# Block-sparse attention with a gated output layer: rebuilt on head pairs over 128 partitions, with the gate's convolution as matrix products

## The chip, the cores and the metric

One NeuronCore of one Trainium2 chip runs the program. It has four engines that compute: TensorE (PE; its weight loads are shown apart as PEld), VectorE (DVE), ScalarE (ACT) and GpSimd (POOL). SyncE (SP) issues the transfers between DRAM and the on-chip memory SBUF. Matrix products land in PSUM, eight banks of 128 partitions x 2 KB, from which DVE and ACT read. The metric is the device time of one execution in microseconds. TensorE's clock has two levels, 1.2 and 2.4 GHz; the profile prints the granted share, 0.50 or 1.00, or a mean over a stretch.

## The reference, cut to what matters

```python
# q, k, v: (4, 8, 768, 64); chunks of 32 keys, so 24 chunks; 6 are kept for each query
k_min, k_max = min and max of k over each chunk
ub = sum over d of maximum(q * k_min, q * k_max)          # a bound per query and chunk
ub = where(chunk is not in the future, ub, -1e9)
top_chunks = argsort(ub)[..., -6:]
scores = q @ k.T / 8
mask = (key's chunk in top_chunks) & (key is not in the future)
attn = softmax(where(mask, scores, -1e9)); x = attn @ v    # heads side by side: (4, 768, 512)
# then, on x
gate_pre = sum over k in 0..4 of conv_w[k] * x shifted by 4-k rows   # causal convolution per channel
out = (sigmoid(gate_pre) * (x @ w_val)) @ w_out            # 512 x 512 each
```

## The kernel before

The kernel walks over 16 pairs of heads (4 batches, 4 pairs each). For a pair, `p13_k` transposes the keys of each head on TensorE, 64 columns at a time (12 float32 transposes, L165), copies them to float16 on ACT (L167) and takes the minimum and maximum of each chunk on DVE (L169, L173). `p13_q` transposes the queries (12 more, L195) and writes each result three times from ACT: as it is, with negative values cut off, and as float16 (L197, L199, L201). The bound is then one float32 product per head and query tile (L205, 12 products of 24 columns, each of which runs as two rows of the profile).

`p48_a` adds the causal fill (L213), finds the eight largest values (L216) and compares with the sixth (L221, on POOL for one head and on DVE for the other). `p48_b` transposes the choice (`selT`, L241, L244) into 24 further rows of the contraction, so that a chunk that is not kept gets -30. `qk` computes the scores as 24 products of 256 columns into banks `psbg` (L255), takes the exponential on ACT 512 columns at a time (L259, 12 per pair), and multiplies the diagonal blocks with a mask on DVE (L262, L264). `av` multiplies with the values (L273, 42 products per pair), and for each of the 12 query tiles divides by the sum (L277, L278, DVE). Six float32 transposes (L302) and two ACT copies (L304) write `xT`.

The gated layer follows per batch: `moe_gate` is the convolution, one product and four multiply-adds of 768 elements on DVE (L314, L318), then the sigmoid on ACT (L322); `moe_val` (L331, L336) and `moe_out` (L344, L350, L351) are the two 512 x 512 layers. They are handed out over the pairs that follow the batch; what is left of the last batch runs at the end.

Buffers come from tile pools, and a scheduler of the framework sets the order on each engine and puts in the waits. Every engine works through its own queue in order, so a waiting instruction holds all behind it. The four banks `psbg` serve transposes, scores and both layers in turn.

## Time and profile before

| | before |
|---|---|
| three timed runs, us | 481.65, 481.69, 481.94 (median 481.69) |
| profiled execution, first to last instruction | 479.9 us |
| PE busy | 366.2 us, 76% |
| DVE busy | 342.4 us, 71% |
| ACT busy | 291.3 us, 61% |
| POOL busy | 42.5 us, 9% |

The profile is of one execution, and its span runs from the first to the last instruction; the page gives no other time of that execution. The median of the timed runs is 1.8 us above the span. Busy time of PE holds the modelled ends of pipelined products, so that start-to-start distances in the timeline price a product better than the mean length of one. The granted clock is read by stretch, since it moves between its two levels many times.

### The profile page before, as it was taken

The page shows a single profiled execution, that of the slowest core. Times are in us where ns is not written, and L with a number is a line of the kernel's source. Part 1 is how long each engine was busy: PE and PEld are TensorE (multiplying, and loading weights), DVE is VectorE, ACT ScalarE, POOL GpSimd, SP SyncE. Part 2 cuts the span into 40 slices and gives each one's busy share as a digit, 9 for nine tenths or more (in the row PEclk, how much of TensorE's full clock was granted, in tenths as well). Part 3 has the DMA queues.
Part 4 walks back from the last instruction along what each step waited for, and adds up shares of the span by engine and source line. Part 5 has one row for each costly group of instructions (what it writes and reads, how often), then busy time and mean ns, then how long its engine had stood idle before and what let it go on. Part 6 is the DMA issues. An engine that isn't in the chain of part 4 may idle for free.

```text
span 479.9 us, 7043 instructions
## 1 busy us (share of the span) xinstructions
PE 366.2 (76%) x2240; PEld 256.1 (53%) x2240; DVE 342.4 (71%) x1345; ACT 291.3 (61%) x548; POOL 42.5 (9%) x132
## 2 busy tenths in 40 slices
PE   0589797888688778778977878777877858587794
PEld 0467576666465646545645556545545645364441
DVE  0465967677796668889577869789786777857671
ACT  3665664556677346767565756576767765662742
POOL 0012010200100101100100102010101001010000
PEclk9955955555565657868587657859796756657588
DMA  7973221212120041203123040303232000000023
GB/s 195 206 141 57 47 54 34 66 33 67 33 68 0 3 98 34 66 20 108 29 87 87 1 99 17 85 1 102 63 100 66 1 1 1 1 0 23 23 89 132
DMA packets 83173, 28.08 MB, mean 59 GB/s; under 512 B 78688, under 2 KB 79040, under 8 KB 83136
## 3 DMA queue, kind: packets, MB, share of 16 engines
q1 hardware_dynamic: 83136, 27.63, 24.0%
q8 instruction: 18, 0.29, 0.3%
q14 instruction: 19, 0.16, 0.1%
HBM read 21.33 MB, written 6.29 MB: 58 GB/s over the span
## 4 chain that ended last, share of the span: by engine, by line
PE 54%; DVE 21%; ACT 16%; issue 4%; SPq 2%; DMA 1%; ACTq 0%; DVEq 0%
PE ps_ub L205 13%; PE psbg L255 12%; PE psbg L331 5%; PE ps_av L273 5%; PE psbg L344 5%; PE psbg L195 4%; ACT PT L259 4%; DVE gp L318 3%; ACT aq L199 3%; DVE onat L278 3%; PE pst L165 3%; PE psbg L302 3%; ACT aq L197 3%; DVE uth L244 2%; PE psbg L241 2%
## 5 line engine op out<-in xcount | busy, mean ns | idle before, releaser
L259 ACT ACTIVATE PT<-psbg 128x512 f16<-128x512 f32 x192 | 101.8, 609 | 55.1 <-PE psbg L255 52.6
L255 PE MATMUL psbg<-uth,KE 88*128 88x256 f16 x384 | 95.1, 392 | 17.6 <-DVE uth L244 8.1
L273 PEld LDWEIGHTS <-PT 128*128 128x128 f16 x672 | 57.2, 120 | 46.9 <-issue 33.6
L205 PEld LDWEIGHTS ps_ub<-kmmc,aq 128*128 128x128 f32 x384 | 71.2, 282 | 14.6 <-ACT aq L199 7.1
L273 PE MATMUL ps_av<-vaug,PT 128*128 128x65 f16 x672 | 65.5, 222 | 16.8 <-DVE onat L278 15.6
L205 PE MATMUL ps_ub<-kmmc,aq 128*128 128x24 f32 x384 | 73.0, 343 | 6.8 <-DVE kmmc L183 3.4
L255 PEld LDWEIGHTS <-KE 88*128 88x128 f16 x384 | 48.6, 137 | 39.6 <-issue 24.0
L318 DVE SCALAR_TENSOR_TENSOR gp<-xT,cwT,gp 128x768 f32<-128x768 f16 x64 | 64.8, 1012 | 0.7
L277 DVE RECIPROCAL rcp<-ps_av 128x1 f32<-128x1 f32 x192 | 32.0, 167 | 43.6 <-PE ps_av L273 40.6
L195 PE MATMUL psbg<-ident,qnat 128*64 128x128 f32 x192 | 43.0, 349 | 19.2 <-DVE kmn L173 6.6
L197 ACT ACTIVATE aq<-psbg 64x384 f32<-64x384 f32 x64 | 30.9, 482 | 38.6 <-PE psbg L195 27.3
L278 DVE TENSOR_SCALAR onat<-ps_av,rcp 128x64 f32<-128x64 f32 x192 | 52.9, 276 | 1.3
L221 POOL TENSOR_SCALAR selpair<-mub,top 128x24 f32<-128x24 f32 x96 | 32.7, 353 | 174.2 <-DVE top L216 173.7
L244 DVE TENSOR_SCALAR uth<-psbg 24x384 f16<-24x384 f32 x64 | 35.3, 551 | 17.6 <-PE psbg L241 16.1
L195 PEld LDWEIGHTS psbg<-ident,qnat 128*64 128x64 f32 x192 | 22.4, 138 | 33.6 <-issue 8.4
L165 PE MATMUL pst<-ident,knat 128*64 128x128 f32 x96 | 21.1, 330 | 24.9 <-DMA qnat<-in_q_dram 15.3
L302 PE MATMUL psbg<-ident,onat 128*128 128x128 f32 x96 | 35.2, 384 | 3.7 <-DVE onat L278 3.3
L331 PE MATMUL psbg<-xT,wval_sb 128*128 128x384 f16 x128 | 34.6, 416 | 2.6 <-ACT xT L304 1.8
L344 PE MATMUL psbg<-wout_sb,gv 128*128 128x512 f16 x96 | 31.2, 446 | 5.4 <-ACT xT L304 4.7
L304 ACT ACTIVATE xT<-psbg 128x384 f16<-128x384 f32 x32 | 15.7, 489 | 28.7 <-PE psbg L302 26.8
L199 ACT ACTIVATE aq<-psbg 64x384 f32<-64x384 f32 x64 | 30.9, 484 | 0.7
L350 ACT ACTIVATE osb<-psbg 128x512 f32<-128x512 f32 x24 | 14.2, 595 | 27.1 <-PE psbg L344 21.7
(40 smaller groups left out, 468.1 us busy)
## 6 DMA issues: line engine op xcount, KB each, us to landing
knat<-in_k_dram SPq DMA_DIRECT2D x32, 192.0 KB, 3.0
qnat<-in_q_dram SPq DMA_DIRECT2D x32, 192.0 KB, 3.1
vnat<-in_v_dram SPq DMA_DIRECT2D x32, 192.0 KB, 3.0
out_dram<-osb SPq DMA_DIRECT2D x24, 256.0 KB, 2.0
w<-in_moe_w_val_dram SPq DMA_DIRECT2D x1, 1024.0 KB
w<-in_moe_w_out_dram SPq DMA_DIRECT2D x1, 1024.0 KB
KE<-echunk SPq DMA_DIRECT2D x4, 36.0 KB
cwT<-in_moe_conv_w_dram SPq DMA_DIRECT2D x5, 2.0 KB, 6.4
```

Source lines behind the costliest of these rows:

```text
L195: nc.tensor.transpose(out=pt[0:64, tl * 128:(tl + 1) * 128], in_=qnat[:, hh, t, :], identity=ident)
L197: nc.scalar.activation(out=aq[64:128, hh, w * 384:(w + 1) * 384], in_=pt[0:64, 0:384], func=AF.Copy)
L199: nc.scalar.activation(out=aq[0:64, hh, w * 384:(w + 1) * 384], in_=pt[0:64, 0:384], func=AF.Relu)
L205: nc.tensor.matmul(out=ps_ub[:, hh, it * NCH:(it + 1) * NCH], lhsT=aq[:, hh, it * 128:(it + 1) * 128], rhs=kmm[:, hh], start=True, stop=True)
L255: nc.tensor.matmul(out=pq[:, half * 256:(half + 1) * 256], lhsT=ke[:, hh, jt * 128:(jt + 1) * 128], rhs=uth[:, hh, w * 256:(w + 1) * 256], ...
L259: nc.scalar.activation(out=pw[:, 2 * a:2 * a + 2, :].rearrange("p a b -> p (a b)"), in_=pq[:, :], func=AF.Exp)
L273: nc.tensor.matmul(out=pav, lhsT=pw[:, jt, qh * 128:(qh + 1) * 128], rhs=vaug[:, hh, jt, :], start=(jt == 0), stop=(jt == qt))
L278: nc.vector.tensor_scalar(out=onat[:, qt, hh * 64:(hh + 1) * 64], in0=pav[:, 0:D], scalar1=r, scalar2=None, op0=ALU.mult)
L302: nc.tensor.transpose(out=pt[:, qtl * 128:(qtl + 1) * 128], in_=onat[:, qt, :], identity=ident)
L318: nc.vector.scalar_tensor_tensor(out=gp, in0=xT[:, slot, ki:ki + S], scalar=cwT[:, ct, ki:ki + 1], in1=gp, op0=ALU.mult, op1=ALU.add)
L331: nc.tensor.matmul(out=pv[:, 0:384], lhsT=wval_sb[:, ct, et * 128:(et + 1) * 128], rhs=xT[:, slot0 + ct, 4 + sw * 384:4 + (sw + 1) * 384], ...
L344: nc.tensor.matmul(out=po[:, :], lhsT=gv_tiles[et][:, sti * 128:(sti + 1) * 128], rhs=wout_sb[:, et, :], start=(et == 0), stop=(et == NCT ...
```

## The change

A pair of heads now lies side by side in 128 partitions. Six transposes bring the keys of both heads, six the queries. ACT writes one float32 copy of the queries; POOL makes the two float16 copies and DVE the one without negative values. The bound is a product with a block matrix `KB` that holds both heads (48 columns), in two parts that add up in PSUM, for 5 of 6 query tiles, since the first tile has no more than four chunks to choose from. The choice is one comparison of 240 columns, and its transposes are float16.

Scores are packed so that nearly all columns are causal ones: 10 banks of 512 columns and one of 256 per pair, in three banks of their own (`ps_s`). The diagonal blocks are cleared by POOL (`affine_select`) and no longer by DVE. The result of `av` fills one bank per head and is divided by two instructions. The transposes to `xT` are float16, and DVE copies them.

The convolution is 20 products of 384 columns per channel block, with diagonal matrices that hold each weight as a float16 high part and a float16 rest; POOL builds them once. The sigmoid is written with tanh. The output layer's factor 0.5 sits in the last copy.

Three stages run side by side: attention of pair i, choice of pair i+1, keys and queries of pair i+2; `merge` spreads their steps. Keys and queries of the first pair are loaded ahead of the other inputs, and the weights are cast on POOL.

```diff
     nc.sync.dma_start(out=ident, in_=ident_dr.ap())
+    load_kq(0)
+    for i in range(3):
+        for hh in range(2):
+            nc.sync.dma_start(out=KE[i][HP[1 - hh], hh, :], in_=e_dr.ap())
+    nc.sync.dma_start(out=cfill, in_=cfill_dr.ap())
...
+        def khalf(w):
+            pt = bank([128, HB])
+            for tl in range(3):
+                nc.tensor.transpose(out=pt[:, tl * 128:(tl + 1) * 128],
+                                    in_=kn[:, 3 * w + tl, :], identity=ident)
+            sl = slice(w * HB, (w + 1) * HB)
+            for hh in range(2):
+                nc.scalar.activation(out=ke[HP[hh], hh, sl], in_=pt[HP[hh]],
+                                     func=AF.Copy, scale=0.125)
+            cs = slice(w * 12, (w + 1) * 12)
+            ptc = pt.rearrange("p (c t) -> p c t", t=CH)
+            nc.vector.tensor_reduce(out=kmx[:, cs], in_=ptc, axis=AX.X, op=ALU.max)
...
+            sl = slice(w * HB, (w + 1) * HB)
+            nc.scalar.activation(out=q32[:, sl], in_=pt, func=AF.Copy)
+            for hh in range(2):
+                nc.gpsimd.tensor_copy(out=qu[HP[hh], hh, sl], in_=q32[HP[hh], sl])
+            a = max(w * HB, 128)
+            nc.vector.tensor_scalar(out=rq[:, a:(w + 1) * HB], in0=q32[:, a:(w + 1) * HB],
+                                    scalar1=0.0, scalar2=None, op0=ALU.max)
+
+        def vcast():
+            for hh in range(2):
+                nc.gpsimd.tensor_copy(out=va[:, hh, :, 0:D],
+                                      in_=vn[:, :, hh * 64:(hh + 1) * 64])
...
+            for it in range(1, NT):
+                ts = slice(it * 128, (it + 1) * 128)
+                nc.tensor.matmul(out=pu[:, it - 1, :], lhsT=rq[:, ts], rhs=kb[:, 0, :],
+                                 start=True, stop=False)
+                nc.tensor.matmul(out=pu[:, it - 1, :], lhsT=q32[:, ts], rhs=kb[:, 1, :],
+                                 start=False, stop=True)
+            nc.vector.tensor_tensor(out=mub.rearrange("p i c -> p (i c)"),
+                                    in0=pu.rearrange("p i c -> p (i c)"),
+                                    in1=cfill, op=ALU.add)
...
+        def cmp():
+            nsv = ns.rearrange("p i (s c) -> p i s c", s=2)
+            nc.vector.tensor_tensor(
+                out=nsv[:, :, :, 0:NCH],
+                in0=mub.rearrange("p i (s c) -> p i s c", s=2),
+                in1=top8[:, :, :, 5:6].to_broadcast([128, SELT, 2, NCH]),
+                op=ALU.is_lt)
...
+            pt = bank([128, SELT * 128], F16)
+            for i in range(SELT):
+                nc.tensor.transpose(out=pt[:, i * 128:(i + 1) * 128], in_=ns[:, i, :],
+                                    identity=identh)
+            for hh in range(2):
+                nc.vector.tensor_copy(out=qu[CP[hh], hh, 128:S], in_=pt[CP[hh], :])
...
+    BANKS = [
+        [(0, 0, 256, 512)],
+        [(0, 0, 0, 256), (256, 4, 512, 256)],
+        [(0, 1, 256, 512)],
+        [(0, 1, 128, 128), (128, 3, 384, 384)],
+        [(0, 2, 256, 512)],
+    ]
...
+        def tri(pt, col, n):
+            ap = pt[:, col:col + n * 128].rearrange("p (a b) -> p a b", a=n)
+            nc.gpsimd.affine_select(out=ap, in_=ap, pattern=[[0, n], [1, 128]],
+                                    compare_op=ALU.is_ge, fill=0.0, base=0,
+                                    channel_multiplier=-1)
+
+        def score(hh, bi):
+            pq = bank([128, 512], FP, "s", 3)
+            for col, jt, q0, n in BANKS[bi]:
+                nc.tensor.matmul(out=pq[:, col:col + n],
+                                 lhsT=ke[KP[hh], hh, jt * 128:(jt + 1) * 128],
+                                 rhs=qu[KP[hh], hh, q0:q0 + n], start=True, stop=True)
+            pt = ppool.tile([128, 512], F16, tag=f"P{hh}{bi}", name=f"P{hh}{bi}")
+            nc.scalar.activation(out=pt, in_=pq, func=AF.Exp)
+            for part in BANKS[bi]:
+                keep(hh, pt, *part)
+            if bi == 1:
+                ap = pt.rearrange("p (a b) -> p a b", a=2)[:, :, 0:128]
+                nc.gpsimd.affine_select(out=ap, in_=ap, pattern=[[0, 2], [1, 128]],
+                                        compare_op=ALU.is_ge, fill=0.0, base=0,
...
+        def av(hh):
+            pav = bank([128, NT, D + 1], FP, "av", 2)
...
+                    nc.tensor.matmul(out=pav[:, qt, :], lhsT=where[hh, jt, qt],
+                                     rhs=va[:, hh, jt, :], start=(jt == 0), stop=(jt == qt))
+            nc.vector.reciprocal(out=rcp[:, hh, :], in_=pav[:, :, D])
+            nc.vector.tensor_tensor(
+                out=onat[:, :, hh * 64:(hh + 1) * 64], in0=pav[:, :, 0:D],
+                in1=rcp[:, hh, :].unsqueeze(2).to_broadcast([128, NT, D]), op=ALU.mult)
...
+            pt = bank([128, S], F16)
+            for qt in range(NT):
+                nc.tensor.transpose(out=pt[:, qt * 128:(qt + 1) * 128], in_=onat[:, qt, :],
+                                    identity=identh)
+            nc.vector.tensor_copy(out=xT[:, slot, 4:4 + S], in_=pt)
...
-        gp = mpool.tile([128, S], FP, tag=f"gp{ct}", name=f"gp{ct}")
-        nc.vector.tensor_scalar(
-            out=gp, in0=xT[:, slot, 0:S], scalar1=cwT[:, ct, 0:1],
-            scalar2=None, op0=ALU.mult)
-        for ki in range(1, KSZ):
-            nc.vector.scalar_tensor_tensor(
-                out=gp, in0=xT[:, slot, ki:ki + S], scalar=cwT[:, ct, ki:ki + 1],
-                in1=gp, op0=ALU.mult, op1=ALU.add)
-        g = mpool.tile([128, S], FP, tag=f"gate{ct}", name=f"gate{ct}")
-        nc.scalar.activation(out=g, in_=gp, func=AF.Sigmoid)
-        gate_tiles[ct] = g
+        g = mpool.tile([128, S], FP, tag=f"g{ct}", name=f"g{ct}")
+        for w in range(2):
+            pg = bank([128, HB])
+            n = 0
+            for ki in range(KSZ):
+                for part in range(2):
+                    nc.tensor.matmul(out=pg, lhsT=diag[:, ki * NCT + ct, part, :],
+                                     rhs=xT[:, slot, w * HB + ki:w * HB + ki + HB],
+                                     start=(n == 0), stop=(n == 2 * KSZ - 1))
+                    n += 1
+
+            nc.scalar.activation(out=g[:, w * HB:(w + 1) * HB], in_=pg, func=AF.Tanh, scale=0.5)
...
+    def moe_weights():
+        nc.gpsimd.tensor_copy(out=wval_sb, in_=w32[:, 0])
+        nc.gpsimd.tensor_copy(out=wout_sb, in_=w32[:, 1])
...
+        for ki in range(KSZ):
+            i = ki * NCT + ct
+            for part, w in ((0, cwT), (1, cwl)):
+                nc.gpsimd.tensor_scalar(out=diag[:, i, part, :], in0=identh,
+                                        scalar1=w[:, i:i + 1], scalar2=None, op0=ALU.mult)
...
+    merge(kq_steps(0))
+    merge(sel_steps(0), kq_steps(1))
+    for i in range(NPAIR):
+        if i + 2 < NPAIR:
+            load_kq(i + 2)
+            load_v(i + 2)
+        merge(attn_steps(i),
+              sel_steps(i + 1) if i + 1 < NPAIR else [],
+              kq_steps(i + 2) if i + 2 < NPAIR else [],
+              moe[i])
...
```

On PE, around the bound's products of one pair in mid-kernel, before (`ps_ub` is the bank of the bound, `KE` and `uth` are operands of the scores):

```order
L255 MATMUL psbg1_102<-uth_2101,KE0_79 128x256
L195 MATMUL psbg3_104<-ident_70,qnat_2091 64x128 x3
...
L255 MATMUL psbg0_101<-uth_2101,KE0_79 128x256
L205 MATMUL ps_ub_105<-kmmc_2405,aq_2400 128x24 x9
L255 LDWEIGHTS KE0_79
L255 MATMUL psbg3_104<-uth_2101,KE0_79 128x256
```

The same place in the changed kernel, where L207 and L209 alternate five times (`ps_w` are the three common banks, `KB` the block matrix of both heads):

```order
L314 MATMUL ps_w_2653<-identh_74,onat_2419 128x128
L155 MATMUL ps_w_2683<-ident_73,kn_2661 128x128 x3
L207 MATMUL ps_w_2697<-KB1_95,rq_2427 128x48
L209 MATMUL ps_w_2697<-KB1_95,q32_2426 128x48
...
L348 LDWEIGHTS wval_sb_76
L348 MATMUL ps_w_2710<-xT_84,wval_sb_76 128x384
...
L348 MATMUL ps_w_2716<-xT_84,wval_sb_76 128x384
...
L271 MATMUL ps_s_2740<-QU1_89,KE1_86 128x512
```

Nine products of 24 columns (of the pair's twelve) stood between scores; now ten of 48 columns stand between transposes and the value layer.

On POOL, one pair of the changed kernel (`P` are exponentials, `QU` the float16 queries, `VA` the float16 values); before, this engine had two MEMSETs and six TENSOR_SCALARs of 24 columns per pair:

```order
L280 AFFINE_SELECT P01_1218<-P01_1218 128x2x128
L264 AFFINE_SELECT P03_1240<-P03_1240 128x256
L264 AFFINE_SELECT P04_1253<-P04_1253 128x128
L264 AFFINE_SELECT P5_1265<-P5_1265 128x256
L183 CAST QU0_88<-q32_1201 64x384 x2
L190 CAST VA1_92<-vn_1412 128x6x64
L280 AFFINE_SELECT P11_1337<-P11_1337 128x2x128
L264 AFFINE_SELECT P13_1352<-P13_1352 128x256
L183 CAST QU0_88<-q32_1201 64x384 x2
L264 AFFINE_SELECT P14_1365<-P14_1365 128x128
```

Masks that the products of `av` wait for now share one queue with casts for a later pair.

On ACT, around a gate, before (`gp` is the convolution):

```order
L201 ACTIVATE uth<-psbg_102 64x384
L322 ACT_TABLE_LOAD
L322 ACTIVATE gate_1238<-gp_1232 128x768
L259 ACT_TABLE_LOAD
L259 ACTIVATE PT_0_1097<-psbg_101 128x512
```

and in the changed kernel, which has one table load in all:

```order
L181 ACTIVATE q_1677<-ps_w 128x384
L275 ACTIVATE P_1842<-ps_s 128x512
L339 ACTIVATE g_1845<-ps_w 128x384 x2
L275 ACTIVATE P_1932<-ps_s 128x512
```

The table loads around a gate are gone, and the gate reads PSUM.

## Rows read from the trace of the kernel before

**Rows 1.** The page: busy time, share of the span and instructions of each engine.

```profile
PE 366.2 (76%) x2240; PEld 256.1 (53%) x2240; DVE 342.4 (71%) x1345; ACT 291.3 (61%) x548; POOL 42.5 (9%) x132
```

**Rows 2.** Stretches: from:to, length, busy us of PE, PEld, DVE, ACT, POOL, clock, DMA.

```profile
41.30:460.40 419.10, 331.67 (x2069) 231.74 (x2069) 319.41 (x1275) 264.70 (x502) 38.80 (x116) 0.66 0.18 44
346.30:360.00 13.70, 10.02 (x85) 6.54 (x84) 12.17 (x38) 8.89 (x19) 0.94 (x2) 1.00 0.38 108
360.00:363.40 3.40, 1.38 (x10) 0.91 (x9) 3.33 (x6) 3.33 (x7) 0.00 (x0) 1.00 0.79 201
363.40:377.00 13.60, 12.67 (x67) 9.25 (x68) 8.70 (x49) 9.35 (x18) 2.06 (x6) 0.50 0.03 7
458.90:472.00 13.10, 12.31 (x70) 6.35 (x69) 8.60 (x15) 5.39 (x8) 0.00 (x0) 1.00 0.27 104
```

**Rows 3.** Timeline of PE: start us, length us, engine, line, operation, out<-in, shape, count.

```profile
254.93 0.49 PE L195 MATMUL psbg<-ident,qnat 128*64 128x128 f32 x3
255.26 0.27 PE L255 MATMUL psbg<-uth,KE 88*128 88x256 f16 x1
257.67 4.04 PE L205 MATMUL ps_ub<-kmmc,aq 128*128 128x24 f32 x18 [0.63 <-ACT aq L199]
...
274.38 0.36 PE L273 MATMUL ps_av<-vaug,PT 128*128 128x65 f16 x6
274.57 0.27 PE L165 MATMUL pst<-ident,knat 128*64 128x128 f32 x1
...
336.55 2.19 PE L205 MATMUL ps_ub<-kmmc,aq 128*128 128x24 f32 x18 [0.63 <-ACT aq L199]
...
468.00 5.34 PE L344 MATMUL psbg<-wout_sb,gv 128*128 128x512 f16 x24
```

**Rows 4.** Groups of ACT: line, operation, shapes, count | busy us, mean ns | idle before, releaser.

```profile
L259 ACT ACTIVATE PT<-psbg 128x512 f16<-128x512 f32 x192 | 101.8, 609 | 55.1 <-PE psbg L255 52.6 <-ACT xT L304 0.9 <-PE ps_av L273 0.8
L322 ACT ACT_TABLE_LOAD x13 | 16.7, 1283 | 0.2
L304 ACT ACTIVATE xT<-psbg 128x384 f16<-128x384 f32 x32 | 15.7, 489 | 28.7 <-PE psbg L302 26.8 <-PE ps_av L273 1.6
L167 ACT ACTIVATE KE<-psbg 64x384 f16<-64x384 f32 x32 | 14.6, 481 | 17.2 <-PE psbg L165 13.4 <-DVE gv L336 3.3 <-DVE kmx L169 0.4
```

**Rows 5.** Groups of DVE, in the same columns.

```profile
L318 DVE SCALAR_TENSOR_TENSOR gp<-xT,cwT,gp 128x768 f32<-128x768 f16 x64 | 64.8, 1012 | 0.7
L216 DVE MAX8 top<-mub 128x8 f32<-128x24 f32 x192 | 22.8, 170 | 0.0
L169 DVE TENSOR_REDUCE kmx<-psbg 64x12 f32<-64x384 f32 x32 | 17.3, 541 | 2.1 <-ACT KE L167 2.1
L336 DVE TENSOR_TENSOR gv<-psbg,gate 128x384 f16<-128x384 f32 x32 | 17.2, 549 | 2.1 <-PE psbg L331 1.9
L213 DVE TENSOR_TENSOR mub<-ps_ub,cfill 128x144 f32<-128x144 f32 x32 | 9.0, 301 | 28.2 <-PE ps_ub L205 28.2
```

**Rows 6.** The value cast on DVE, all instructions: ns min/median/max; its longest in the timeline.

```profile
L154 DVE TENSOR_SCALAR vaug<-vnat x32: 339/347/548, 17.7 to 408.8; 128x384 f16<-128x384 f32 x32
...
57.41 0.55 DVE L154 TENSOR_SCALAR vaug<-vnat 128x384 f16<-128x384 f32 x1
...
57.68 0.51 POOL L159 MEMSET selpair<- 128x240 f32 x1
```

**Rows 7.** Groups of POOL, in the columns of rows 4.

```profile
L221 POOL TENSOR_SCALAR selpair<-mub,top 128x24 f32<-128x24 f32 x96 | 32.7, 353 | 174.2 <-DVE top L216 173.7
L158 POOL MEMSET selpair<- 128x240 f32 x16 | 4.8, 298 | 209.3 <-PE psbg L241 159.9 <-DVE PT L264 35.1 <-DVE uth L244 14.0
```

**Rows 8.** The chain that ended last, in order of time; last, a row of the timeline.

```profile
15.35 1.46 PE pst L165 x6
...
41.24 1.59 PE psbg L255 x6
...
460.46 0.49 ACT L304 ACTIVATE xT<-psbg 128x384 f16<-128x384 f32 x1
```

447 lines of the change are left out of this document (174 added, 273 removed).

## The prediction

> **What bounds the kernel now.** I read the page's busy times first, then the stretches with their clock, then the timeline of PE. On the page no engine is full: PE 76%, DVE 71%, ACT 61% [rows 1]. The stretches tell why. Between the first score and the last `xT`, 419 us for 16 pairs or 26.2 us each, the mean clock is 0.66 [rows 2], so (1 - 0.66)/0.5 = 68% of that time is at half clock. In a stretch at half clock PE is busy 12.67 of 13.60 us (93%) and DVE only 8.70. In one at full clock it is the other way: DVE 12.17 of 13.70 (89%), PE 10.02. In the 3.4 us after it DVE and ACT are both busy for 3.33 us, PE for 1.38, and then the clock is down [rows 2]. So two limits take turns: at half clock PE sets the pace; at full clock DVE with ACT does, PE runs thin, and the clock falls again. In the tail, where long products follow one another (PE 12.31 of 13.10 us), it stays at 1.00 [rows 2].
>
> Prices of PE at full clock come from start-to-start distances [rows 3]. A float32 transpose: (255.26 - 254.93)/3 = 0.110 us. A product of `av` with 65 columns: (274.57 - 274.38)/6 = 0.032. The 24 products of 512 columns at the end: 5.34/24 = 0.222, or 0.434 ns a column; shorter float16 products are priced by columns. A row of the bound: 2.19/18 = 0.122, and 4.04/18 = 0.224 at half clock.
>
> A pair before is then 36 transposes 3.96, 24 rows of the bound 2.93, scores 24 x 256 columns 2.67, `av` 42 x 0.032 = 1.34, value layer 8 x 384 columns 1.33, output layer 6 x 0.222 = 1.33: 13.6 us at full clock, 27.1 at half. DVE has 319.4/16 = 20.0 us a pair [rows 2]. With the shares seen, half-clock time costs 27.1/0.93 = 29.2 us a pair and full-clock time 20.0/0.89 = 22.4. Mixing rates, 0.68/29.2 + 0.32/22.4 = 0.0376 pairs per us, or 26.6 us a pair, against 26.2 measured. The same sum serves for the changed kernel.
>
> **The change, PE.** Transposes: 12 float32 ones 1.32, 11 float16 ones of 128 columns at about 0.06 (between `av`'s 0.032 and 0.110) 0.66. Bound: 10 products, 20 rows; at 0.122 they cost 2.44. The columns double, which costs nothing if the weight load of 128 columns covers it, and up to 4.9 if time follows columns; I take 2.44, because 24 columns at 0.434 ns a column would explain only 0.010 of the 0.122. Scores: 5376 columns, 2.33. `av` as before 1.34. Convolution, new: 20 products of 384 columns, 3.33. Value and output layers as before, 1.33 each. Sum 14.1 us a pair, 225 us in all: half a microsecond more than before. The change does not relieve PE; the convolution spends what the transposes save.
>
> **The change, DVE.** Gone: the convolution (four multiply-adds of 1012 ns per block [rows 5]), the masks, the narrow divisions. Left for a pair [rows 5 and 6]: 4 reductions of 541 ns 2.16; 10 MAX8 1.70; the fill and the comparison, 240 columns each, between 0.301 and 0.549, at 0.40 each; two copies of the choice with 640 columns, from 0.30 to 0.81 (0.549 and the slope (549 - 301)/240 = 1.03 ns a column), 1.2 for both; 2 divisions 1.1 and 2 reciprocals 0.34; the copy to `xT`, 0.55 to 0.95, at 0.75; 2 products with the gate 1.1; cut-off queries 0.347 for 384 columns, 0.6 for both; five small ones for `KB` at 0.17 to 0.35, 1.2. Ends 9.6 and 12.5; I take 11.0, against 20.0.
>
> **The change, ACT.** 10 exponentials 6.09, one of 256 columns about 0.4, 4 copies of keys 1.92, 2 of queries 0.98, 2 tanh on 384 columns 0.98 (the copy's row, since no tanh has run), 1.5 output copies 0.91 [rows 4]: 11.3. Gone are two thirds of the copies of queries, the copies to `xT`, and the table loads of 1283 ns around the gates (13 in the row shown, 12 more at L259 going back).
>
> **The change, POOL.** It has 13 wide instructions a pair. The rows know 0.298 us for a 240-column MEMSET and 0.353 for a 24-column compute instruction [rows 7]; masks and casts do not occur. Low end: 13 x 0.298 = 3.9. High end, 0.353 and 298/240 = 1.24 ns for each further column: 0.80 for six casts, 0.64 for five masks of 256, 0.48 for two of 128, or 9.0. I take 8, the compute row being nearer than a MEMSET. The first four pairs carry 40 diagonals (0.48 each, 4.8 a pair) and two weight casts (2.9 each): up to 15 there, level with PE, hidden by the order's slack of three stages, 0.5 to 1 us each if not. DVE and POOL disturb each other: the value cast takes 347 ns as a rule and 548 where a MEMSET of POOL, itself 0.51 instead of 0.298, lies beside it [rows 6 and 7]. Seven DVE instructions a pair (`rq`, comparison, `KB`) could lose 0.2 to 0.8 us when POOL is busy, which is half the time: 0.7 to 2.8, so DVE up to 13.8, still within PE's 14.4 below.
>
> The Trainium skill ("SBUF — State Buffer", Who interferes with whom) calls this an exclusive lock: a DVE instruction in a two-port mode, or with two SBUF inputs, and a GpSimd instruction block one another for a whole instruction. The case of 548 ns agrees; by that rule the upper 2.8 us would hold, and the sum would not move, since PE stays the longest.
>
> **Sum.** At full clock PE is now the busiest (14.1; ACT 11.3, DVE 11, POOL 8), so it is no longer thinned by DVE.
>
> Head: the first transposes start at 15.35 and the first score at 41.24 [rows 8]. Keys and queries are now second in the load queue, so transposes can start near 5.5. From there: 12 transposes at half clock 2.6, the last reductions and `KB` 3.5, cut-off 0.6, bound 20 x 0.224 = 4.5, fill, MAX8, comparison 2.5, transposes and copies 1.8: first score at 21.
> Tail: before, last `xT` at 460.95 to the end at 479.9, 19 us. Now convolution 3.3, value layer 32 x 0.167 = 5.3, output layer 24 x 0.222 = 5.3, and the last copies, stores and hand-overs about 6 (6.6 after the last product before: 473.34 to 479.9): 20.
> Middle: PE's 225 less head (24 transposes, one bound, 5.4) and tail (14.0) is 206, or 12.9 us a pair. At full clock, at the 89% that the pace-setter reached, 14.4 us; at half clock 25.7/0.93 = 27.7. The share of half clock is the unknown, with 0 and 0.68 as ends. I take 0.30: the load that thinned PE halves (20.0 to 11), the bound is 20 rows of 48 columns instead of 24 of 24 before which the clock fell, and each pair has a dense block of 3.3 us like the tail's. Then 0.70/14.4 + 0.30/27.7 = 0.0594, or 16.8 us a pair, 269 for 16.
> 21 + 269 + 20 = 310 us of span. With the 1.8 us by which the median lies above the span: **312 us**. With shares 0 and 0.5 the middle is 230 and 303: 273 to 346 is the forecast's own range.
>
> **Rivals.**
> *The clock stays as it is now.* The bound still stands as one block, and such a block runs thin: 18 rows of 24 columns took 2.19 us at full clock [rows 3], the time of some 5000 columns of the output layer. If each pair's block ends the full clock as before, the share stays 0.68: 21.4 us a pair, 342, total 385. Against it: DVE and ACT no longer fill the full-clock stretches.
> *Hand-overs thin PE.* Three score banks, each held for a product (0.222) and an exponential (0.609 [rows 4]): if PE waits out the difference at 11 banks (4.2 us) and for exponential and mask twice before `av` (2.4 us), a pair at full clock costs 12.9 + 6.6 = 19.5, total 355. For it: ACT waits 52.6 us for scores and DVE long for `av` now; against it: other products stand between the scores in the order.
> *Half clock throughout.* 27.7 x 16 + 43 = 486, slower than before, since PE's columns have not become fewer. It decides only from a share of about 0.99; the tail and every dense stretch speak against it.
> *POOL sets the pace, slower than before.* Its masks stand between exponential and `av`. The middle would have to exceed 482 - 43 = 439 us, 27.4 a pair or 2.1 us for each of 13 instructions, six times the row of 0.353. At 2.3 us: 30 us a pair, 523 in all.
>
> The Trainium skill ("GPSIMD Engine Reference", Elementwise — side-by-side cycle accounting) gives about 12 cycles an element for branching on data, at 1.2 GHz; were the masks such code, 1536 columns a pair would cost an estimated 15.4 us and POOL about 20, a total of 364 (inside the range below). No row here shows a mask on POOL.
>
> **How the numbers follow.** Forecast 0.56; clock as now 0.19; hand-overs 0.17; half clock throughout 0.04; POOL 0.04. A measurement of this kernel tells 0.2%, about 1 us, from no change. Faster: 0.92; slower: 0.07, most of the last two cases; the same: 0.01. The range from 270 to 388 takes in the forecast, the clock's case and the hand-overs, less what the unknown prices add beyond their ends: about 8 in 10.
>
> **What would show it.** Right: a mean clock near 0.85 in the middle, PE above 80% busy, near 17 us from one pair's first score to the next, DVE and ACT each near 11 us a pair, first score near 21 us. Wrong: a mean clock under 0.7; POOL busy above 70% with PE waiting on masks; DVE's mean lengths well above the rows because POOL holds it; rows of the bound at twice 0.122.

## The result and the profile after

The changed kernel takes **293.81 us** (median of 4 runs, 293.45 to 294.23) against 481.81 for the kernel before: a ratio of 0.607 (95% interval 0.604 to 0.610). The forecast was 312 with a range from 270 to 388. The profiled execution has a span of 292.5 us. Runs more than 1.5% above the fastest of their kernel are left out of the medians, ranges and ratios below.

The page of the changed kernel: busy time of each engine with its share of the span, then the granted clock in 40 slices, then the engines' shares of the chain that ended last.

```profile
PE 241.3 (82%) x2161; PEld 171.6 (59%) x2161; DVE 155.2 (53%) x522; ACT 160.2 (55%) x329; POOL 121.8 (42%) x261
...
PEclk9999975956999999999999999999999999999999
...
PE 66%; POOL 12%; ACT 10%; issue 3%; SPq 3%; DVE 2%; DMA 2%; ACTq 0%; POOLq 0%
```

Against [rows 1], DVE fell from 342.4 to 155.2 us, ACT from 291.3 to 160.2, POOL rose from 42.5 to 121.8. PE fell from 366.2 to 241.3, though by the prediction's prices it has half a microsecond more to do in each pair: what fell is the time at half clock.

The stretches of the changed kernel, cut at first scores: the head; pairs 0 and 1 together, then pair 1 alone; pairs 2 to 14; the last pair. Columns as in [rows 2].

```profile
0.00:27.07 27.07, 10.96 (x50) 9.22 (x50) 14.48 (x43) 7.02 (x13) 10.04 (x24) 1.00 1.03 232
...
27.07:73.70 46.63, 27.39 (x218) 18.96 (x219) 15.22 (x61) 17.39 (x36) 37.15 (x68) 0.74 0.58 106
...
48.40:73.70 25.30, 15.18 (x124) 10.27 (x122) 8.31 (x31) 9.30 (x19) 24.69 (x44) 0.69 0.29 63
73.70:260.80 187.10, 175.78 (x1707) 128.40 (x1705) 117.27 (x404) 121.41 (x253) 72.05 (x162) 1.00 0.31 75
...
260.80:273.70 12.90, 12.36 (x113) 7.27 (x110) 3.75 (x9) 8.63 (x17) 2.61 (x7) 1.00 0.22 83
```

The middle is one long stretch at full clock: 13 pairs in 187.1 us, **14.4 us a pair, PE busy 94%** of it (175.78/187.1), DVE 9.0 us a pair, ACT 9.3, POOL 5.5. (A mean: from first score to first score single pairs take 12.4 to 16.9 us, the shortest being the early ones, which have neither value nor output layer yet.) The two limits that took turns in [rows 2] have become one. What is slow now is the beginning: pairs 0 and 1 take 46.6 us, at a mean clock of 0.74, and POOL is busy for 24.69 of the 25.30 us of pair 1.

PE's prices in the middle, at full clock (timeline: start, length, engine, line, operation, out<-in, shape, count; the count's last product ends within the length, so a price is the distance to the next start):

```profile
157.29 2.28 PE L334 MATMUL ps_w<-xT,diag 128*128 128x384 f16 x13
159.41 0.50 PE L314 MATMUL ps_w<-identh,onat 128*128 128x128 f16 x6
...
159.96 0.49 PE L155 MATMUL ps_w<-ident,kn 128*128 128x128 f32 x3
160.29 0.38 PE L271 MATMUL ps_s<-QU,KE 88*128 88x256 f16 x2
...
160.67 0.39 PE L209 MATMUL ps_w<-KB,q 128*128 128x48 f32 x2
```

A product of the convolution costs (159.41 - 157.29)/13 = 0.163 us, a float16 transpose (159.74 - 159.41)/6 = 0.055, a float32 transpose (160.29 - 159.96)/3 = 0.110. From 160.67 to the output layer's product at 162.68 stand 18 rows of the bound: 0.112 each with 48 columns, where rows of 24 columns cost 0.122 before [rows 3].

### The profile page after: what moved, and what is told of

It is laid out like the page before. It is cut to its first block, busy times and chain, and to the rows that moved or that the text cites. A ratio compares the mean times of both kernels' runs of the same rounds, so it can differ in the third digit from the quotient of the medians.

```text
span 292.5 us, 5928 instructions
## 1 busy us (share of the span) xinstructions
PE 241.3 (82%) x2161; PEld 171.6 (59%) x2161; DVE 155.2 (53%) x522; ACT 160.2 (55%) x329; POOL 121.8 (42%) x261
## 4 chain that ended last, share of the span: by engine, by line
PE 66%; POOL 12%; ACT 10%; issue 3%; SPq 3%; DVE 2%; DMA 2%; ACTq 0%; POOLq 0%
PE ps_w L334 17%; PE ps_s L271 10%; POOL diag L379 7%; PE ps_av L304 6%; PE ps_w L348 6%; PE ps_w L359 6%; PE ps_w L209 6%; ACT P L275 5%; PE ps_w L207 5%; PE ps_w L155 4%; PE ps_w L178 2%; POOL QU L183 2%; PE ps_w L314 2%; ACT KE L159 2%; ACT osb L362 1%
## 5 line engine op out<-in xcount | busy, mean ns | idle before, releaser
L275 ACT ACTIVATE P<-ps_s 128x512 f16<-128x512 f32 x160 | 87.8, 606 | 57.1 <-PE ps_s L271 56.8
L271 PE MATMUL ps_s<-QU,KE 88*128 88x512 f16 (+5 forms) x224 | 54.9, 336 | 7.1 <-ACT P L275 4.1
L264 POOL TENSOR_SCALAR_AFFINE_SELECT P<-P 128x256 f16<-128x256 f16 (+1 forms) x80 | 29.0, 364 | 71.1 <-ACT P L275 58.3
L334 PE MATMUL ps_w<-xT,diag 128*128 128x384 f16 x320 | 57.8, 331 | 0.0
L304 PE MATMUL ps_av<-VA,P 128*128 128x65 f16 x672 | 33.4, 196 | 21.9 <-POOL P L264 19.9
L304 PEld LDWEIGHTS <-P 128*128 128x128 f16 x672 | 28.4, 99 | 32.0 <-POOL P L264 26.2
L159 ACT ACTIVATE KE<-ps_w 64x384 f16<-64x384 f32 x64 | 31.0, 485 | 26.9 <-PE ps_w L155 26.5
L183 POOL CAST QU<-q 64x384 f16<-64x384 f32 x64 | 35.1, 548 | 24.6 <-ACT q L181 22.7
L334 PEld LDWEIGHTS <-diag 128*128 128x128 f16 x320 | 31.0, 99 | 21.4 <-issue 1.9
L209 PE MATMUL ps_w<-KB,q 128*128 128x48 f32 x160 | 32.3, 285 | 0.0
L163 DVE TENSOR_REDUCE kmx<-ps_w 128x12 f32<-128x384 f32 x32 | 17.8, 555 | 26.7 <-ACT KE L159 26.6
L207 PE MATMUL ps_w<-KB,rq 128*128 128x48 f32 x160 | 31.2, 278 | 0.0
L207 PEld LDWEIGHTS ps_w<-KB,rq 128*128 128x128 f32 x160 | 25.9, 202 | 0.3
L209 PEld LDWEIGHTS ps_w<-KB,q 128*128 128x128 f32 x160 | 25.7, 202 | 0.0
L190 POOL CAST VA<-vn 128x384 f16<-128x384 f32 x32 | 16.5, 516 | 20.4 <-PE ps_av L304 12.9
```

The lines of the kernel that those rows point to most:

```text
L159: nc.scalar.activation(out=ke[HP[hh], hh, sl], in_=pt[HP[hh]], func=AF.Copy, scale=0.125)
L183: nc.gpsimd.tensor_copy(out=qu[HP[hh], hh, sl], in_=q32[HP[hh], sl])
L207: nc.tensor.matmul(out=pu[:, it - 1, :], lhsT=rq[:, ts], rhs=kb[:, 0, :], start=True, stop=False)
L209: nc.tensor.matmul(out=pu[:, it - 1, :], lhsT=q32[:, ts], rhs=kb[:, 1, :], start=False, stop=True)
L264: nc.gpsimd.affine_select(out=ap, in_=ap, pattern=[[0, n], [1, 128]], compare_op=ALU.is_ge, fill=0.0, base=0, channel_multiplier=-1)
L271: nc.tensor.matmul(out=pq[:, col:col + n], lhsT=ke[KP[hh], hh, jt * 128:(jt + 1) * 128], rhs=qu[KP[hh], hh, q0:q0 + n], start=True, stop=True)
```

## Where the sum missed

| part | forecast | measured |
|---|---|---|
| first score | 21 | 27.1 |
| pairs 0 and 1 | 33.6 | 46.6 |
| the other 14 pairs | 235.2 | 200.0 |
| tail after the last `xT` | 20 | 18.8 |
| span | 310 | 292.5 |

So two errors of opposite sign: the other 14 pairs came out 35 us better, the head and the first two pairs 19 us worse. The experiments ask three things. Is it the relief of DVE, or the new block of products on PE, that brought the full clock? What makes the first pairs slow? Does PE really set the pace of the middle?

The early waits of PE in the changed kernel (engine, line, released by: us in total, times, longest), from 27 to 74 us; the second line is the costliest in the whole middle, from 73.7 to 260.8:

```profile
PE ps_av L304 <- POOL P L264: 16.1, 3, 8.6
...
PE ps_s L271 <- ACT P L275: 3.8, 13, 0.4
```

POOL's groups in the changed kernel (line, operation, shapes, count | busy us, mean ns | idle before, releasers):

```profile
L264 POOL TENSOR_SCALAR_AFFINE_SELECT P<-P 128x256 f16<-128x256 f16 (+1 forms) x80 | 29.0, 364 | 71.1 <-ACT P L275 58.3 <-ACT P L295 11.4
...
L280 POOL TENSOR_SCALAR_AFFINE_SELECT P<-P 128x256 f16<-128x256 f16 x32 | 13.1, 408 | 31.4 <-ACT P L275 31.3
L379 POOL TENSOR_SCALAR diag<-identh,cwT 128x128 f16<-128x128 f16 x20 | 12.9, 647 | 0.0
L379 POOL TENSOR_SCALAR diag<-identh,cwl 128x128 f16<-128x128 f16 x20 | 12.0, 601 | 0.1
L366 POOL CAST wval_sb<-w 128x2048 f16<-128x2048 f32 x1 | 2.1, 2067 | 0.0
```

The 40 diagonals cost 0.60 to 0.65 us each and come ten in a row; a causal mask that stands behind them in POOL's queue would be late, and `av` does wait up to 8.6 us for one. The experiments on the first two pairs, further down, begin with that suspicion.

## Experiments: what the convolution on PE does

**The convolution back on VectorE.** Everything else of the change stays.

```diff
-                    nc.tensor.matmul(out=pg, lhsT=diag[:, ki * NCT + ct, part, :],
-                                     rhs=xT[:, slot, w * HB + ki:w * HB + ki + HB],
...
+        for ki in range(1, KSZ):
+            nc.vector.scalar_tensor_tensor(
+                out=gp, in0=xT[:, slot, ki:ki + S],
+                scalar=cwT[:, ki * NCT + ct:ki * NCT + ct + 1],
+                in1=gp, op0=ALU.mult, op1=ALU.add)
...
+        nc.scalar.activation(out=g, in_=gp, func=AF.Tanh, scale=0.5)
```

> One part of the change undone: the convolution is on DVE again (one product and four multiply-adds of 768 elements per block), tanh reads SBUF, no diagonals are built; all else as in the changed kernel. PE loses 3.26 us a pair (14.4 to about 11.1), DVE gains 4.7 (to about 14.3). Theory (the clock stays full because DVE no longer thins PE): DVE becomes the pace-setter again, 14.3/0.89 = 16 us a pair, half clock comes back in part: 300 to 325 us although the early loss from the diagonals is gone. Rival (the convolution on PE is plain cost, DVE had room for it at 53% busy): PE sets 11.1 to 12.5 us a pair at full clock: 245 to 262.

Measured: 333.7 us (331.1 to 335.7), ratio 0.697 (0.679 to 0.715). That is 40 us more than the changed kernel and 9 above the upper end of the theory, although 16 x 3.26 = 52 us of products have left PE. The stretch of its pairs 3 to 13 (11 pairs, 18.8 us each):

```profile
78.20:285.20 207.00, 166.47 (x1240) 121.62 (x1240) 150.90 (x406) 105.65 (x210) 74.40 (x141) 0.73 0.25 62
```

PE's two largest waits in it (engine, line, released by: us in total, times, longest):

```profile
PE ps_w L230 <- DVE NS L221: 18.7, 10, 5.8
PE ps_s L268 <- DVE QU L233: 10.4, 10, 1.8
```

The mean clock is down to 0.73, and PE stands still at the choice of chunks (`NS`), 1.9 us each time and once in nearly every pair. Among PE's waits in the middle of the changed kernel none is on `NS` (the smallest listed there is 0.7 us in all). The rival is out: fewer columns on PE did not make the kernel faster. DVE is not full either: 13.7 of 18.8 us a pair. So moving the convolution to PE may do two things: it takes work off DVE, and it lies over the chain bound, six largest, comparison, transposes, in which PE otherwise waits. This run undoes both at once. Part of the wait on `NS` may also come from the convolution's own steps, which stand in DVE's queue ahead of the comparison.

**The kernel before with its convolution on PE** (diagonals by VectorE, and the tanh form of the gate), nothing else of the change.

```diff
-            nc.vector.scalar_tensor_tensor(
-                out=gp, in0=xT[:, slot, ki:ki + S], scalar=cwT[:, ct, ki:ki + 1],
-                in1=gp, op0=ALU.mult, op1=ALU.add)
...
+                    nc.tensor.matmul(out=pg[:, 0:384], lhsT=diag[:, ki * NCT + ct, part, :],
+                                     rhs=xT[:, slot, w * 384 + ki:w * 384 + ki + 384],
+                                     start=(n == 0), stop=(n == 2 * KSZ - 1))
```

> One part of the change done alone, in the kernel before: the convolution as 20 products with diagonals per block on PE (diagonals built on DVE), and tanh for the sigmoid. DVE falls from 20.0 to 15.3 us a pair, PE rises from 13.6 to 16.9 at full clock. Theory (relief of DVE and the dense block raise the clock): half-clock share 0.3 instead of 0.68, 22 us a pair, about 415 us (390 to 440), clock above 0.8. Rival (PE only gets more to do, the clock stays at 0.66): 26.8 us a pair, 480 to 500.

Measured: 457.6 us (456.4 to 459.0), ratio 0.960 (0.950 to 0.969), between the two ranges. The kernel before ran from 474.9 to 486.5 us beside it, so the size of the gain is loose. Its 16 pairs, from the first score to the last `xT`:

```profile
42.90:437.00 394.10, 345.82 (x2392) 233.49 (x2391) 259.21 (x1202) 235.00 (x496) 41.23 (x118) 0.80 0.19 48
```

The clock rose from 0.66 [rows 2] to 0.80, as the mechanism wants, but a pair there has 13.6 + 3.3 = 16.9 us of products at full clock. By the prediction's own mixing sum, with 88% busy (345.82/394.1) and a half-clock share of 0.40, a pair takes 24.0 us; 24.6 were measured. So the small gain fits the same sum, with the measured clock and busy share put in afterwards: the better clock is nearly used up by the 3.3 us of new products. By the prediction's prices the rebuilding on head pairs takes out nearly as much time of PE (2.8 us a pair) as the convolution puts in.

**The bound as narrow products.** The changed kernel, with 20 float32 products of 24 columns per pair in place of 10 of 48.

```diff
-                nc.tensor.matmul(out=pu[:, it - 1, :], lhsT=rq[:, ts], rhs=kb[:, 0, :],
-                                 start=True, stop=False)
...
+                for s in range(2):
+                    cs = slice(s * NCH, (s + 1) * NCH)
+                    nc.tensor.matmul(out=pu[:, it - 1, cs], lhsT=rq[:, ts], rhs=kb[:, 0, cs],
+                                     start=True, stop=False)
```

> The changed kernel with the bound as 20 products of 24 columns a pair instead of 10 of 48 (each head by itself): 40 rows of the profile a pair instead of 20. PE gets 20 rows more at 0.112 us, 2.24 a pair. Theory (a block of narrow products does not end the full clock where PE is dense around it): clock stays 1.00 in the middle, time up by 16 x 2.24 = 36 less what early waits hide: 322 to 332 us. Rival (each such block brings half clock back, as in the kernel before): half of each pair at half clock, 380 us or more.

Measured: 355.8 us (351.8 to 356.3), ratio 0.744 (0.729 to 0.758): 62 us more, nearly double what the rows alone cost, and between the ranges of theory and rival. A stretch of some nine pairs:

```profile
160.00:330.00 170.00, 166.35 (x1380) 121.37 (x1378) 82.31 (x279) 88.09 (x181) 48.91 (x111) 0.86 0.21 55
```

Four rows of one bound in it, from the timeline:

```profile
194.57 0.38 PE L209 MATMUL ps_w<-KB,rq 128*128 128x24 f32 x2
...
196.80 0.38 PE L209 MATMUL ps_w<-KB,rq 128*128 128x24 f32 x2
...
198.03 0.60 PE L211 MATMUL ps_w<-KB,q 128*128 128x24 f32 x2
198.45 0.60 PE L209 MATMUL ps_w<-KB,rq 128*128 128x24 f32 x2
```

Twenty rows from 194.57 to 196.80 are 0.112 each, the same as with 48 columns: the doubled columns cost nothing. Doubling the count costs 20 x 0.112 x 16 = 36 us. The rest is the clock: from 198 on a row costs 0.21, in the record the clock is half from 197.8 to 204.6, and such a fall stands in nearly every pair, each time at this block. PE is busy for 98% of the stretch, and the clock fell all the same. The mean clocks of the four runs, 0.85 to 0.90 against 0.95 to 0.96 in the changed kernel, say the same. In the changed kernel the block is half as long, with twice the columns, and the clock stays. Which of the two saves it, this run doesn't separate. Still, the prediction's rival "the clock stays as it is now" was right about the place, and its remedy lay in a part of the change that I had priced for its time alone.

**The sigmoid back.** The changed kernel with a sigmoid in place of the tanh, and the product and the output copy that go with it as before.

```diff
-            nc.scalar.activation(out=g[:, w * HB:(w + 1) * HB], in_=pg, func=AF.Tanh, scale=0.5)
+            nc.scalar.activation(out=g[:, w * HB:(w + 1) * HB], in_=pg, func=AF.Sigmoid)
...
```

> The changed kernel with a sigmoid in place of the tanh, so that table loads come back on ScalarE (in the kernel before two a pair and more). Theory, ScalarE has 9.3 us of work in a 14.4 us pair and TensorE sets the pace: about 2.6 us of loads a pair disappear in ScalarE's idle time, 294 to 304 us. Rival, a load stands between scores and exponentials and holds TensorE up each time: 2.6 x 16 = 41 us more, 325 to 340, and more if the clock falls.

Measured: 304.5 us (303.8 to 304.8), ratio 0.630 (0.627 to 0.633), 10.7 us more and just above the theory's band (294 to 304). Its table loads, by the groups of ACT:

```profile
L339 ACT ACT_TABLE_LOAD x15 | 19.2, 1283 | 0.3
L275 ACT ACT_TABLE_LOAD x14 | 18.0, 1283 | 5.6 <-PE ps_s L271 5.5
```

The one pair in the middle that fell to half clock, as a stretch:

```profile
114.50:136.80 22.30, 21.25 (x158) 15.53 (x158) 10.57 (x34) 11.69 (x23) 7.41 (x17) 0.69 0.28 62
```

29 loads, 37 us on ACT, cost 10.7 us of time, and of these some 6 lie in this one pair (22.3 instead of 16.1). Most of the rest is hidden. So the tanh was worth about 4%, not more.

## Experiments: the first two pairs

**The diagonals on VectorE.**

```diff
-                nc.gpsimd.tensor_scalar(out=diag[:, i, part, :], in0=identh,
+                nc.vector.tensor_scalar(out=diag[:, i, part, :], in0=identh,
```

> One edit to the changed kernel: the 40 diagonal matrices are built on DVE instead of POOL. Theory: POOL was full from 39 to 71 us with diagonals of 0.6 us each, PE waited for masks behind them and lost its full clock there; the first two pairs took 21.3 and 25.3 us where later ones without the output layers take 12.3 to 13.0. So about 20 us go: 274 us (270 to 279), and the clock is 1.00 from about 30 us on. Rival: those pairs are slow because of the loads (DMA share 0.93 to 1.30 until 48 us); then 288 to 294.

Measured: 287.8 us (285.9 to 289.9), ratio 0.604 (0.594 to 0.613). By the medians 6 us less, at the rival's end; the interval of the ratio overlaps that of the changed kernel (0.604 to 0.610), so the gain is not clear of noise, and the pairs tell more than the total. Pair 0 and pair 1 of it as stretches:

```profile
27.30:50.20 22.90, 16.18 (x103) 12.17 (x104) 12.95 (x44) 8.08 (x17) 8.17 (x16) 1.00 0.91 161
50.20:66.90 16.70, 14.78 (x117) 11.78 (x115) 12.01 (x53) 9.13 (x19) 5.90 (x13) 1.00 0.32 72
```

Two rows of its timeline:

```profile
43.52 1.89 POOL L367 CAST wout_sb<-w 128x2048 f16<-128x2048 f32 x1
43.54 1.92 DVE L379 TENSOR_SCALAR diag<-identh,cwT 128x128 f16<-128x128 f16 x1
```

A diagonal costs 0.245 us on VectorE (median of 40) instead of 0.60 on GpSimd. Pair 1 went from 25.3 to 16.7 us, and the waits of `av` on masks with it (17.9 us in pairs 0 and 1 together, now 1.0). Pair 0 did not gain (21.3 to 22.9), and pair 2 lost (12.4 to 14.8, its mean clock 0.77 instead of 1.00): GpSimd's diagonals were the cause of pair 1's loss only, and in their new place one of them is held up by GpSimd's cast for 1.92 us. (The 1.00 of these two pairs stands ahead of the first change that the record holds and is not the speed: in pair 0 the 20 rows of the bound, from 32.78 to 36.91, took 0.21 us each, the price at half clock, and those of pair 1, from 51.50 on, took as long.)

**Three moves at once:** the weights cast by ScalarE in eight pieces, the diagonals two at a time, and pair 0's bound and choice ahead of pair 1's keys.

```diff
-    merge(sel_steps(0), kq_steps(1))
+    s0, k1 = sel_steps(0), kq_steps(1)
+    for s in s0[:3] + [k1[0], s0[3]] + k1[1:]:
+        s()
...
-        nc.gpsimd.tensor_copy(out=wval_sb, in_=w32[:, 0])
-        nc.gpsimd.tensor_copy(out=wout_sb, in_=w32[:, 1])
+                moe[2 + i].append(lambda i=i, dst=dst, c=c: nc.scalar.activation(
+                    out=dst[:, c, :], in_=w32[:, i, c, :], func=AF.Copy))
...
-        moe[i].append(lambda i=i: moe_diag(i))
+        moe[i] += [lambda i=i, ki=ki: moe_diag(i, ki) for ki in range(KSZ)]
```

> The kernel with the diagonals on VectorE, and three more moves in the early part: the output weights are cast by ScalarE in eight pieces in pairs 2 and 3 instead of by GpSimd in pair 1, the diagonals come two at a time between other steps, and pair 0's bound and top six go ahead of pair 1's keys. Theory, the early loss (first score at 27.3, first two pairs 23.0 and 16.7 where later ones take 14.4) is hand-overs that these three cause: first score at 20 to 22, first two pairs 17 and 14.5, 274 us (270 to 280). Rival, the early part is slow because TensorE's products take twice as long there until it has been busy for a while, whatever feeds it: first score at 23 or later, first pair 21 or more, 283 to 288 us.

Measured: 280.7 us (279.4 to 283.5), ratio 0.582 (0.577 to 0.586), with the next kernels the fastest that compute the whole; half of what the theory wanted. The first score moved from 27.3 to 18.8 us, earlier than the 20 to 22 it said. Pairs 0 and 1 took 20.9 and 17.4 us, close to what the rival said. In the record the clock was half from 32.3 to 49.3.

**The loads of the weights behind those of pair 2.**

```diff
+        if i == 0:
+            nc.sync.dma_start(out=w32[:, 0], in_=moe_w_val.rearrange("(ct c) e -> c ct e", c=128))
+            nc.sync.dma_start(out=w32[:, 1], in_=moe_w_out.rearrange("(et e) o -> e et o", e=128))
```

> The kernel with the three moves in the early part, and the 2 MB of output weights loaded behind pair 2's keys, queries and values instead of ahead of them. There TensorE stood still for 5.7 us at pair 2's keys, and its clock was half for the 17.1 us that followed (32.3 to 49.3). Theory, the halt costs twice, itself and the half clock behind it: pair 0 takes 15 to 17 us instead of 20.9 and pair 1 14 to 16 instead of 17.4, 273 us (270 to 276) against 280.7. Rival, the clock falls at that place for another reason (the chain bound, top six, selection of pair 1, in which TensorE waits 3.6 us more): no half clock goes, 278 us or more.

Measured: 280.3 us (279.9 to 280.6), ratio 0.584 (0.580 to 0.588), no change. The expectation rested on a misreading: the wait of 5.7 us in the trace of the kernel with the three moves stands at the very start, for pair 0's keys, not at pair 2's. So the theory fell, and what remains is the rival's place. Three rows of PE in this kernel:

```profile
35.27 0.72 PE L231 MATMUL ps_w<-identh,NS 128*128 128x128 f16 x5 [5.01 <-DVE NS L222]
...
51.60 0.71 PE L231 MATMUL ps_w<-identh,NS 128*128 128x128 f16 x5 [4.63 <-DVE NS L222]
52.10 5.91 PE L332 MATMUL ps_w<-xT,diag 128*128 128x384 f16 x20
```

PE waits 5.0 us in pair 0 and 4.6 in pair 1 for the comparison, the same wait as with the convolution on VectorE. In later pairs the convolution stands there; in pair 0 there is none yet, and in pair 1 the 20 products stand behind the wait and run mostly at half clock (5.91 us, against 3.26 in the middle).

> The same change of the order of loads in the kernel that uses only the high float16 part of the convolution's weights (the rest of each weight is left out). Theory: 7 us less than its 261.0, 254 us (250 to 257), with pair 0 at 15 to 17 us. Rival: 258 us or more.

The same order of loads with the high part of the weights alone: 260.7 us (259.8 to 261.5), ratio 0.543 (0.540 to 0.545), against 261.0 without it. No change here either.

**Products that are thrown away, laid over these two waits.**

```diff
+        for _ in range(n):
+            nc.tensor.matmul(out=pf, lhsT=zero[:, 0:128], rhs=zero, start=True, stop=True)
...
+            if p in (1, 2):
+                filler(24)
```

> The kernel with the changed order of loads (280.5 us), and 24 products of 384 columns of zeros put on TensorE ahead of the transposes of the selection of pairs 1 and 2, where it stood still for 5.0 and 4.6 us (the products are thrown away). Theory, the middle keeps its full clock because the convolution lies under just these waits, and the first two pairs lose it because they have none: with something to multiply the clock stays at 1.00 from about 26 us on, pair 0 takes 17 to 18.5 us (18.7) and pair 1 16 to 18 (21.2), 276 us (274 to 278), faster with 48 products more. Rival, the clock of these pairs does not depend on the wait: 24 products at half clock take 7.8 us, 3 us more than the wait in each pair, 284 us or more.

Measured: 280.7 us (278.9 to 282.5), ratio 0.580 (0.573 to 0.586): the same time as without the 48 products. Rows of PE, the first two from the bound that runs within pair 0, the others in pair 1:

```profile
25.49 0.39 PE L215 MATMUL ps_w<-KB,q 128*128 128x48 f32 x2
...
27.28 0.39 PE L215 MATMUL ps_w<-KB,q 128*128 128x48 f32 x2
...
48.30 4.07 PE L143 MATMUL ps_w<-zero 128*128 128x384 f16 x24
...
52.95 3.42 PE L342 MATMUL ps_w<-xT,diag 128*128 128x384 f16 x20
```

Its pair 0, its pair 1, then pairs 2 and 3 together as stretches:

```profile
18.30:37.50 19.20, 15.38 (x127) 10.59 (x128) 15.47 (x60) 12.06 (x25) 7.96 (x18) 1.00 1.14 261
37.50:56.50 19.00, 17.33 (x151) 12.27 (x151) 14.41 (x55) 11.01 (x23) 6.96 (x15) 0.91 0.72 141
56.50:88.50 32.00, 27.61 (x247) 19.41 (x245) 18.73 (x60) 18.17 (x39) 11.28 (x26) 0.89 0.39 81
```

Half of the theory held: from the bound that runs within pair 0 on (rows of 0.112 us, 25.49 to 27.28) the clock is full to the end of that pair, where it fell to half without the products, and 0.91 in pair 1, and the convolution takes 3.42 us instead of 5.91. The other half failed. Pairs 0 and 1 take 38.2 us instead of 39.9, and pairs 2 and 3 give it back (31.9 instead of 28.4, with two short falls of the clock). So in these pairs the clock alone is not what costs the time. DVE is busy for 15.47 of 19.20 us in pair 0, with the diagonals between its steps; that PE at full clock only waits sooner for what DVE hands over fits this, but is not shown.

> The same 48 products in the kernel with only the high float16 part of the convolution's weights (the rest of each weight is left out), and 12 more ahead of the first transposes, while TensorE waits 5.7 us for pair 0's keys. Theory: 5 us less in the first two pairs as above, and the first score at 15.5 to 17 instead of 18.2 since the first transposes and the bound no longer run at half clock: 254 us (251 to 257). Rival: the first score stays at 18 or later and the pairs as slow as they were, 261 us or more.

Measured: 260.8 us (260.7 to 262.4), ratio 0.540 (0.536 to 0.543), as without any of the 60 products. With the 12 products ahead of the first transposes, the transposes of the queries ran at full clock (three at 7.63 in 0.52 us, against 0.87 in the kernel with the three moves alone); from 9.7 to 26.7 the recorded clock is half, and the first score came at 18.9 instead of 18.2. That answers for the rival.

## Experiments: does PE set the pace of the middle

**Only the high half of the convolution's weights**, with the diagonals on VectorE, and then with the three early moves as well.

```diff
-                for part in range(2):
+                for part in range(1):
...
```

> The kernel with the diagonals on VectorE, and of the convolution's weights only the high float16 part: it leaves out the rest of each weight, ten of the twenty products of 384 columns per pair (1.63 us of 3.26 at full clock). Theory, TensorE sets the pace of the middle at 14.4 us a pair: 16 x 1.63 = 26 us less than the 287.8 us of the kernel with both parts, so 262 us (256 to 268). Rival, what TensorE does there is cover and the pace is set by the hand-overs: under 8 us less, 280 or more; or the thinner TensorE falls back to half clock, and the time goes up.

> Both at once: only the high float16 part of the convolution's weights (the rest of each weight is left out), and the three moves in the early part. Theory, the two add up, since one takes work from TensorE in every pair and the other takes waits out of the first two: 262 - 13 = 249 us (242 to 256). Rival, with 12.8 us of products a pair TensorE waits for others and its clock falls in places: 262 or more.

Measured: 268.1 us (266.8 to 269.4), ratio 0.555 (0.550 to 0.560), and 261.0 us (260.3 to 261.2), ratio 0.540 (0.537 to 0.543). Each is 19.7 us less than its counterpart with both parts, not 26, and the second lies 5 us above its theory's range. The second pair of kernels shows the reason. Twelve pairs with both parts, as a stretch:

```profile
71.50:246.50 175.00, 163.97 (x1583) 119.28 (x1580) 108.75 (x371) 112.68 (x235) 65.69 (x148) 1.00 0.30 73
```

PE's wait for masks in it:

```profile
PE ps_av L304 <- POOL P L264: 3.0, 6, 0.7
```

The same twelve pairs with the high part alone:

```profile
68.30:229.60 161.30, 146.34 (x1467) 107.56 (x1465) 108.16 (x372) 110.70 (x235) 65.56 (x148) 1.00 0.32 80
```

And PE's wait for masks there:

```profile
PE ps_av L302 <- POOL P L262: 7.8, 15, 0.8
```

PE lost 1.47 us of work a pair, the pair became 1.14 us shorter (14.58 to 13.44): 78% of the work taken from PE comes back as time, and the rest turns into waits on masks (3.0 to 7.8 us). So PE does set the pace, at 94% busy closely and at 91% already less so. The clock stayed at 1.00 in both, so half of the block of products is enough for it. Whether the relief of DVE would do it with no block at all was not run: the first of the three questions is answered only for both together.

## Why the prediction was right, and by how much it was not

- **The mechanism: right.** PE's work a pair was to stay as it was, DVE's to halve, and PE to set a pace of 14.4 us at full clock. That pace was measured to the tenth, with some luck: PE is busy for 13.5 us a pair in the middle (175.78/13) where the sum had 12.9, and it reaches 94% where I took 89%. Of the other signs named for being right, the clock near 0.85 (1.00), 17 us a pair (14.4), 11 us of DVE and ACT (9.0 and 9.3) and the first score near 21 (27.1) did not come out.
- **The share of half clock: mis-sized.** This term failed: 0.30 was taken between 0 and 0.68, and in the 13 pairs of the middle it is 0 (clock 1.00). Over the whole stretch from the first score to the last `xT` some 24 of 247 us are recorded at half clock, all before 70.8 us; by the rows of the bound, which cost 0.21 us each until 33.1, the first 6 us ran at half too. With 0 the sum gave 273, the range's lower end plus 3. That 312 lies within 6% of 293.8 is therefore luck in part: with the share of the middle the same sum falls 21 us short, and the head and the first two pairs, which it had too cheap, make up for it. Of the three reasons for a fall below 0.68 the first, DVE's load, was not undone alone; undoing the third (the dense block in each pair, which also puts work back on DVE) or the second (the wide bound, which also doubles its rows) brings half clock back into nearly every pair.
- **What the convolution covers: not in the sum.** I priced it as work that spends what the transposes save. It also stands where PE waits for the choice, 1.9 us a time in the run without it.
- **PE's prices: right.** 0.163 us per 384 columns (0.167 taken), 0.055 per float16 transpose (0.06), 0.110 per float32 transpose, 0.112 per row of the bound with doubled columns (0.122, and up to twice that as the bound).
- **DVE and ACT: too dear.** 9.0 and 9.3 us a pair in the middle against 11.0 (ends 9.6 and 12.5) and 11.3. DVE came out below its low end. Neither is in the sum, which goes by PE.
- **POOL: the sum right on the safe side, the cover wrong.** 5.5 us a pair in the middle, within 3.9 to 9.0. A mask of 256 columns takes 0.408 us and all masks of a pair 42.1/16 = 2.6. The diagonals took 0.60 to 0.65, not 0.48, and "hidden by the order's slack" failed: the slack of three stages helps the convolution's weights, but the masks of the same pair stand behind the diagonals in POOL's queue. That was named as the price if the cover is gone, at 0.5 to 1 us each, 20 to 40 us for the 40. On VectorE, where they cost time too, the total is about 6 us lower, and that is not clear of noise; what they cost as such was not measured.
- **The head: 27 instead of 21.** Three rows of the changed kernel tell it:

```profile
14.19 0.88 PE L155 MATMUL ps_w<-ident,kn 128*128 128x128 f32 x3 [4.53 <-DMA kn<-in_k_dram]
...
24.12 2.07 POOL L366 CAST wval_sb<-w 128x2048 f16<-128x2048 f32 x1
24.36 2.04 DVE L185 TENSOR_SCALAR rq<-q 128x384 f32<-128x384 f32 x1
```

The first transposes began at 5.22 (5.5 forecast). But the order puts pair 1's keys ahead of pair 0's bound, and PE waited 4.5 us for their load; then `rq`, which takes 0.34 to 0.66 us in all later pairs, took 2.04 beside POOL's cast. The wait for the keys could be read from the order before the run; with the bound moved ahead and the cast given to ScalarE the first score came at 18.8.

"SBUF — State Buffer" of the Trainium skill (Who interferes with whom) describes the lock by which two such instructions hold each other up for a whole instruction. The traces agree twice: 2.04 us beside 2.07, and 1.92 beside 1.89 where a diagonal on VectorE otherwise takes 0.245. The 0.7 to 2.8 us a pair that the prediction allowed for this do not show in the total of the middle: DVE has 9.0 us a pair there, below the low end without them.

The other rule weighed, of the Trainium skill ("GPSIMD Engine Reference", Elementwise — side-by-side cycle accounting), is about 12 cycles an element for branching on data. For a mask of 256 columns it would give an estimated 2.6 us; 0.408 were measured, so the masks do not run at that price.

- **The tail: right.** 18.8 us against 20.
- **The rivals.** Hand-overs (355) cost PE 6% of the middle. The clock as now (385) did not come, though a bound of narrow products would have brought part of it. POOL as pace-setter was true of pair 1 alone.

What stays open: why pairs 0 and 1 still take 38 to 40 us in every version with both parts and the diagonals on VectorE (34 to 37 with the high part alone, which has half the diagonals), against 29 for two later pairs. It is not the clock alone, not GpSimd's diagonals and casts, and not the order of the weights' loads. The chain of DVE steps with the diagonals between them is the candidate left. The shorter times with half the diagonals speak for it, and so does the run with the convolution on VectorE, which builds no diagonals: 18.6 and 14.1 us, 32.6 for both. But these runs have fewer products in pair 1 as well, and the candidate was not tested by itself.

## What to carry to other kernels

When two limits take turns, sum up the pair for the pace-setter at full clock first. Here the next engine had a third of the time to spare (9.3 of 14.4 us), and the share of half clock fell to nothing, so that end deserved more weight than a middle value. It is no guarantee: with the narrow bound the others had as much to spare, and the clock fell. Work moved to the pace-setting engine may be cheap where it lies over a wait of that engine: look for the wait before pricing the work. And set-up work on a side engine is not hidden by slack in its own results; what counts is who stands behind it in the same queue.
